# Making the folded key weights in both row halves on TensorE, with smaller weight loads and a new order

## Chip, cores, metric

The kernel runs on one core of a Trainium2 chip. The metric is device time in microseconds of one launch; a number of runs is given by its median, lowest and highest. Lower is better. Line numbers (L390) are those of the kernel before.

## What is computed

The input x has S = 2048 rows of D = 576. There are 32 heads of 18 columns. Cut to what matters:

```python
def _A_ref(x, wqkv, w_phi, wo):          # token mixer
    q, k, v = split_heads(x @ wqkv)
    pq = einsum("bhsd,hdf->bhsf", q, w_phi)
    pk = einsum("bhsd,hdf->bhsf", k, w_phi)
    phi_q = concat([softmax(pq), softmax(-pq)], -1)
    phi_k = concat([softmax(pk), softmax(-pk)], -1)
    kv = einsum("bhsf,bhsd->bhfd", phi_k, v)
    z  = einsum("bhsf->bhf", phi_k)
    o = (phi_q @ kv) / (phi_q @ z + 1e-6)
    return merge_heads(o) @ wo

def _B_ref(x, w1, b1, w2, b2):           # MLP, 576 -> 4608 -> 576
    return gelu(layernorm(x) @ w1 + b1) @ w2 + b2

h  = x + _A_ref(layernorm(x), ...)
h2 = h + _B_ref(layernorm(h), ...)
```

## The kernel before, in words

The 2048 rows are 16 tiles of 128 rows; two tiles make a pair p (0 to 7), the unit of the first part. The contraction of 576 is cut into KC = 9 chunks of 64. In `lnb` the chunks of a pair's two tiles stand beside each other, so that one 128x128 transpose brings chunk c of tile 0 to partitions 0 to 63 and of tile 1 to partitions 64 to 127 (`lnT`). Every projection (`project`, L390) then runs two rows of 64 partitions at once, one tile in each, 18 matmuls with 288 columns; its weights are needed in both halves of the partitions.

The feature weights are folded: wk times the block-diagonal w_phi (`bd`, made by `spread`, L198, on GpSimd from w_phi and a mask). For that wk is transposed on TensorE in five column groups (`flip_mm` L334, evicted by `flip_ev` L340 into `wT`), and `fold_mm` (L350) multiplies in 128-row chunks, six matmuls each, evicted by `fold_ev` (L361) into `wkp` for keys and `wqp` for queries. A 128-row chunk holds two 64-row chunks, each in one half; so the other halves are filled by copies (`swap` L368, `swap_last` L371, on GpSimd, VectorE and ScalarE for keys; `swap_q` by DMA for queries), and key and query projections pick their chunks in the order CROSSED. The value weights `wv` are loaded into the lower half and copied to the upper half on GpSimd (`copy_values`, L158).

Order of the first part, per pair and half i of the columns:
- `stats` (L271 to L274, VectorE), `power` (L279, GpSimd), `centre` (L245, GpSimd) and `scale` (L291 on VectorE or L251 on ScalarE) normalise the rows; the turn to `lnT` is done by TensorE for pairs 0 and 1 (`turn_x_mm`, L308, evicted at L315 and L317) and by a transposing DMA for the rest (`turn_dma`, L298).
- `key_mm` and `value_mm` (L390), `key_exp` (two exponentials, L412, ScalarE), `value_ev` (L400), `key_sum` (reduce and reciprocal, L441 and L443, VectorE), `key_weigh` (two multiplies of a tile, L447, GpSimd), and `sums` (L482, TensorE), which adds the pair to `acc_kv`, a PSUM tile that lives through the whole first part.
- After the last `sums`, `table` (L495, L499) makes the masked matrix `kvm` with `window_masks` (L217, L221); queries run through the same steps (`query_*`), are turned by DMA (`turn_q`), and `combine_mm` (L565), `divide` (L575, L578), the turn of o, `residual_mm` (L612), `residual_add` (L625, L626), `second` (L631, L233, L235) and `rescale` (L239) lead to the MLP's input `ln2T`.

PSUM in the first part: the pool `two` has three buffers of two banks, taken in turn by every product and transpose; `pn` has one.

Then come eight MLP blocks of 256 rows (`mlp`): `up` makes 18 pairs of hidden chunks (`pair`, L1027; gelu on ScalarE, L1051) and `down` multiplies back (L1072; last add L1076). Between them stand the next rows' combines and residuals, at places given by `rises` and `falls` (index of the pair, or of the matmul). In the first block `up` begins with the first of the two row tiles alone for `first` = 3 pairs, before the second tile's turn has arrived.

The order on each engine is written out by hand: the list of calls L682 to L1008 is the program order, and every engine runs its own instructions in that order and waits at each for what it reads. Loads are issued by SP (`load_*`), apart from x tiles 0 and 1 and w_phi, which ScalarE issues first of all (L162 to L170). SP's queue also holds the transposing DMAs. Eight completion semaphores serve the DMAs of SP and ScalarE in turn, so each DMA waits for the one eight places ahead of it.

## Time and profile before

| what | value |
|---|---|
| three runs: median (lowest to highest) | 402.1 us (401.37 to 405.12) |
| the profiled execution: time, span | 403.26 us, 401.5 us |
| mean granted clock of TensorE in it | 0.991 |
| first matmul starts | 1.42 us |
| first key projection starts | 19.04 us |
| last sums end | 72.6 us |
| first whole pair of the MLP starts | 95.93 us |
| last matmul ends | 398.1 us |

The profile gives for each engine the time in which it is busy: PE is TensorE's matmuls, PEld its weight loads, DVE VectorE, ACT ScalarE, POOL GpSimd, SP SyncE; a "q" behind a name is the queue that issues. A line of the timeline has start, duration, engine, line, operation, output and inputs, count, and in brackets the idle time before it with what ended it; instructions of one kind that follow each other are merged, and the shape shown is that of the first. The granted clock is the share of TensorE's clock that was let through.

### The profile page before, as it was taken

The page shows a single profiled execution, that of the slowest core. Times are in us where ns is not written, and L with a number is a line of the kernel's source. Part 1 is how long each engine was busy: PE and PEld are TensorE (multiplying, and loading weights), DVE is VectorE, ACT ScalarE, POOL GpSimd, SP SyncE. Part 2 cuts the span into 40 slices and gives each one's busy share as a digit, 9 for nine tenths or more (in the row PEclk, how much of TensorE's full clock was granted, in tenths as well). Part 3 has the DMA queues.
Part 4 walks back from the last instruction along what each step waited for, and adds up shares of the span by engine and source line. Part 5 has one row for each costly group of instructions (what it writes and reads, how often), then busy time and mean ns, then how long its engine had stood idle before and what let it go on. Part 6 is the DMA issues. An engine that isn't in the chain of part 4 may idle for free.

```text
span 401.5 us, 12158 instructions
## 1 busy us (share of the span) xinstructions
PE 387.7 (97%) x5435; PEld 322.4 (80%) x5435; DVE 166.7 (42%) x353; ACT 186.4 (46%) x399; POOL 124.1 (31%) x139
## 2 busy tenths in 40 slices
PE   7699999988999999999999999999999999999996
PEld 6577777768877898888778888888888888778875
DVE  4898996467118307500750264036205300600000
ACT  2888887765800680077008601840383048106800
POOL 4999899117303302500250034003401100211010
PEclk9899999999999999999999999999999999999999
DMA  8998759999963602350332034004400500120000
GB/s 204 183 172 177 128 108 191 220 202 230 304 82 75 105 4 38 66 77 2 60 65 56 2 75 85 23 3 84 94 3 2 104 16 2 21 56 16 2 16 16
DMA packets 72462, 33.84 MB, mean 84 GB/s; under 512 B 58842, under 2 KB 69338, under 8 KB 72410
## 3 DMA queue, kind: packets, MB, share of 16 engines
q1 hardware_dynamic: 71520, 32.75, 41.6%
q8 instruction: 42, 0.69, 0.7%
q10 hardware_dynamic: 890, 0.32, 0.4%
q14 instruction: 10, 0.08, 0.1%
HBM read 16.53 MB, written 2.36 MB: 47 GB/s over the span
## 4 chain that ended last, share of the span: by engine, by line
PE 86%; DVE 5%; DMA 4%; POOL 1%; ACT 1%; issue 1%; ACTq 0%; SPq 0%; DVEq 0%; POOLq 0%
PE ph L1027 35%; PE po L1072 33%; PE pk L390 7%; PE pa L612 4%; PE pv L390 4%; DMA w<-in_A_w_phi_dram 2%; PE acc_kv L482 1%; PE pn L565 1%; DMA lnT<-shared 1%; DVE st L626 1%; DVE xh L625 1%; DVE shared L239 1%; DVE st L271 1%; PE pT L308 1%; POOL wv L158 1%
## 5 line engine op out<-in xcount | busy, mean ns | idle before, releaser
L1051 ACT ACTIVATE h<-ph,b1col 128x256 bf16<-128x256 f32 x288 | 120.7, 471 | 170.6 <-PE ph L1027 153.7
L1027 PE MATMUL ph<-shared,w 64*128 64x256 bf16 (+1 forms) x2646 | 145.1, 268 | 2.9 <-DVE shared L315 1.1
L1072 PE MATMUL po<-w,h 128*128 128x288 bf16 x1152 | 144.7, 286 | 0.0
L1027 PEld LDWEIGHTS <-w 64*128 64x128 bf16 x2646 | 128.6, 95 | 18.6 <-issue 5.5
L1072 PEld LDWEIGHTS <-h 128*128 128x128 bf16 x1152 | 111.2, 98 | 29.3 <-issue 1.9
L235 POOL TENSOR_TENSOR rs<-va,mhalf 128x1 f32<-128x1 f32 x16 | 8.8, 551 | 173.2 <-DVE va L233 173.2
L625 DVE TENSOR_TENSOR xh<-pa,xh 128x288 bf16<-128x288 f32 x32 | 14.3, 446 | 114.7 <-PE pa L612 114.7
L390 PEld LDWEIGHTS <-lnT 64*128 64x128 bf16 x864 | 42.3, 95 | 12.9 <-issue 1.4
L1076 DVE TENSOR_TENSOR ot<-po,hb 128x288 bf16<-128x288 f32 x32 | 14.5, 454 | 80.6 <-PE po L1072 79.8
L447 POOL TENSOR_TENSOR phiq<-phiq,rk 128x576 bf16<-128x576 bf16 x32 | 36.4, 1164 | 22.2 <-DVE rk L443 22.2
L1062 POOL TENSOR_TENSOR hb<-xh,b2bc 128x576 f32<-128x576 bf16 x16 | 20.4, 1275 | 62.9 <-DVE ot L1076 61.2
L447 POOL TENSOR_TENSOR phik<-phik,rk 128x576 bf16<-128x576 bf16 x32 | 36.3, 1164 | 1.5 <-DVE rk L443 1.3
L441 DVE TENSOR_REDUCE sk<-phik 128x64 f32<-128x1152 bf16 x16 | 21.3, 1332 | 1.9 <-ACT phik L412 1.8
L412 ACT ACTIVATE phiq<-pk 128x576 bf16<-128x576 f32 x32 | 18.6, 651 | 7.5 <-PE pk L390 7.5
L441 DVE TENSOR_REDUCE sk<-phiq 128x64 f32<-128x1152 bf16 x16 | 21.3, 1330 | 0.0
L390 PE MATMUL pv<-wv,lnT 64*128 64x288 bf16 x288 | 20.5, 289 | 0.7 <-POOL wv L158 0.5
L390 PE MATMUL pk<-shared,lnT 64*128 64x288 bf16 x288 | 19.8, 283 | 0.6 <-DMA lnT<-shared 0.4
L412 ACT ACTIVATE phik<-pk 128x576 bf16<-128x576 f32 x32 | 18.8, 664 | 3.3 <-PE pk L390 3.3
L390 PE MATMUL pk<-wqp,lnT 64*128 64x288 bf16 x288 | 19.4, 283 | 0.2 <-DVE xh L625 0.2
L612 PE MATMUL pa<-wo,shared 64*128 64x288 bf16 x288 | 19.0, 283 | 0.0
L443 DVE RECIPROCAL rk<-sk 128x64 f32<-128x64 f32 x32 | 17.7, 553 | 2.2
L612 PEld LDWEIGHTS <-shared 64*128 64x128 bf16 x288 | 14.5, 94 | 3.2 <-issue 0.2
(71 smaller groups left out, 199.5 us busy)
## 6 DMA issues: line engine op xcount, KB each, us to landing
w<-in_B_w_dram SPq DMA_DIRECT2D x24, 432.0 KB, 7.9
...
```

Source lines behind the costliest of these rows:

```text
L390: nc.tensor.matmul(dst[:, a, 0:HALF], lhs[rows, c, :], w[rows, slot, i * HALF : (i + 1) * HALF], start=(n == 0), stop=(n == KC - 1),)
L412: nc.scalar.activation(rows[:, :, i * HH : (i + 1) * HH, s, :], flight[key, p, i][:, :, 0:HALF].rearrange("p a (h f) -> p a h f", f=DH), A ...
L441: nc.vector.tensor_reduce(sk[:, :, :], part_of(dst, i), AX.X, ALU.add)
L443: nc.vector.reciprocal(rk[:, :, :], sk[:, :, :])
L447: eng.tensor_tensor(part, part, flight["r" + key, p, i][:, a, :].rearrange("p (h o) -> p h o", o=1).to_broadcast([P, NH, DH]), ALU.mult,)
L612: nc.tensor.matmul(pa[a], oT[p % 2][rows, c, :], wo[rows, c, cs], start=(c == 0), stop=(c == KC - 1),)
L625: nc.vector.tensor_tensor(xh[:, t, cs], flight["a", p, i][a], xh[:, t, cs], ALU.add)
L1027: nc.tensor.matmul(ph[half][:, cols], w1[p_ // 9][rows, c, p_ % 9 * P : (p_ % 9 + 1) * P], x[rows, c, cols], start=(c == 0), stop=(c == KC ...
L1051: nc.scalar.activation(h1[m // 9][:, m % 9, :], ph[half][:, :], AF.Gelu_apprx_tanh, bias=b1col[:, m : m + 1], scale=1.0,)
L1062: nc.gpsimd.tensor_tensor(hb[:, :], xh[:, t, :], b2bc[:, :], ALU.add)
L1072: nc.tensor.matmul(po[:, :], h1[m // 9][:, m % 9, i_ * P : (i_ + 1) * P], w2[m // 18][:, m % 18, cs], start=(n == 0), stop=(n == NM - 1),)
L1076: nc.vector.tensor_tensor(ot[:, cs], po[:, :], hb[:, cs], ALU.add)
```

## The change

- `load_wk` loads wk's columns in two pieces (254 and 322) and its last 64 rows apart; `load_rows` goes. All are issued by SP, ahead of the x tiles from 2 on.
- w_phi's two DMAs are issued by GpSimd, behind the identity matrix.
- `fold_k_mm` folds keys in nine chunks of 64 rows, each twice with the same operands, once into output partitions 0 to 63 and once into 64 to 127; `fold_k_ev` evicts both at once. The key swaps go, and keys use the plain order of chunks.
- `stats` takes one tile at a time, and the variance plus epsilon is made on GpSimd. `copy_values` copies five or four chunks at a time. `sums` takes one tile at a time. `sk` and `rk` have six buffers instead of three.
- Transposes into the pool `two` take two buffers, one for each part.
- In the first MLP block only one pair begins with the first row tile alone, behind the second tile's turn on TensorE; `enter` of the next rows comes at 60 instead of 64; the second weighing of query pair 3 and its turn move from the end of block 0 into block 1.
- The order of the first part is new throughout. Of it the diff below shows the start, up to the load of the last x tiles, and the end, from the last `sums` on; in the part left out the same steps stand in another order. On SP the order of loads is then: wk pieces, x 2 to 3, x 4 to 7, values 0, x 8 to 11, values 1, wq, the turn of pair 2, five turns of wq, the turn of pair 3, x 12 to 15, and so on.

```diff
@@ -138,11 +138,14 @@
-    def load_rows(dst, src):
-        n = src.shape[1]
-        nc.sync.dma_start(dst[0:64, 4, 0:n], src[512:576, :])
+    def load_wk(part):
+        if part == 0:
+            nc.sync.dma_start(wk[0:KH, 4, :], A_wqkv[512:D, D : 2 * D])
+            return
+        f0, f1 = ((0, 254), (254, D))[part - 1]
         nc.sync.dma_start(
-            dst[:, 0:4, 0:n], src[0:512, :].rearrange("(c p) f -> p c f", p=P)
+            wk[:, 0:4, f0:f1],
+            A_wqkv[0:512, D + f0 : D + f1].rearrange("(c p) f -> p c f", p=P),
         )
...
@@ -153,24 +156,24 @@
             ),
         )
 
-    def copy_values(i, copy):
+    def copy_values(i, part, copy):
         cs = slice(i * HALF, (i + 1) * HALF)
-        copy(wv[KH:P, :, cs], wv[0:KH, :, cs])
+        ks = slice(part * 5, 5 + part * 4)
+        copy(wv[KH:P, ks, cs], wv[0:KH, ks, cs])
 
     wphi_rows = A_w_phi.rearrange("h d f -> (h d) f")
+
+    def load_x(t0, t1):
+        nc.sync.dma_start(xh[:, t0:t1, :], x_v[:, t0:t1, :])
+
     for t in range(2):
         nc.scalar.dma_start(xh[:, t, :], x_v[:, t, :])
 
-    def load_x(t0, t1):
-        nc.sync.dma_start(xh[:, t0:t1, :], x_v[:, t0:t1, :])
-
-    nc.scalar.dma_start(
+    make_identity(nc, ident)
+    nc.gpsimd.dma_start(
         wph[0:126, 0:4, :], wphi_rows[0:504, :].rearrange("(g p) f -> p g f", p=126)
     )
-    nc.scalar.dma_start(wph[0:72, 4, :], wphi_rows[504:576, :])
-    load_rows(wk, A_wqkv[:, D : 2 * D])
-
-    make_identity(nc, ident)
+    nc.gpsimd.dma_start(wph[0:72, 4, :], wphi_rows[504:576, :])
     ones7 = small.tile([P, 7], FP32, name="ones7", tag="ones7")
     nc.gpsimd.memset(ones7[:, :], 1.0)
     nc.gpsimd.memset(mhalf[:, :], -0.5)
...
@@ -263,15 +266,18 @@
     def turned(p):
         return lnT[p // 2][:, p % 2, :, :]
 
-    def stats(p):
-        mv = small.tile([P, 2, 2], FP32, name="mv", tag="mv")
-        for i in range(2):
-            st = small.tile([P, 2, nc.vector.BN_STATS_DIM], FP32, name="st", tag="st")
-            for h in range(2):
-                nc.vector.bn_stats(st[:, h, :], xh[:, 2 * p + i, h * HALF : (h + 1) * HALF])
-            nc.vector.bn_aggr(mv[:, i, :], st[:, :, :])
+    def stats(p, i):
+        if i == 0:
+            moments[p] = [small.tile([P, 2, 2], FP32, name="mv", tag="mv")]
+        mv = moments[p][0]
+        st = small.tile([P, 2, nc.vector.BN_STATS_DIM], FP32, name="st", tag="st")
+        for h in range(2):
+            nc.vector.bn_stats(st[:, h, :], xh[:, 2 * p + i, h * HALF : (h + 1) * HALF])
+        nc.vector.bn_aggr(mv[:, i, :], st[:, :, :])
+        if i == 0:
+            return
         va = small.tile([P, 2], FP32, name="va", tag="va")
-        nc.vector.tensor_scalar(va[:, :], mv[:, :, 1], 1.0, EPS, ALU.mult, ALU.add)
+        nc.gpsimd.tensor_scalar(va[:, :], mv[:, :, 1], 1.0, EPS, ALU.mult, ALU.add)
         moments[p] = [mv, va, None, None]
 
     def power(p):
...
     flight = {}
 
-    def transposes(key, src, home=two, tag="two"):
-        pT = flight[key] = home.tile([P, 16, P], BF16, name="pT", tag=tag)
+    def transposes(key, src, home=None):
+        if home:
+            pT = home.tile([P, 16, P], BF16, name="pT", tag="pn")
+            parts = [pT[:, 0:5, :], pT[:, 8:12, :]]
+        else:
+            parts = [
+                two.tile([P, 5 - e, P], BF16, name="pT", tag="two")[:, :, :] for e in range(2)
+            ]
+        flight[key] = parts
         for c in range(KC):
             nc.tensor.transpose(
-                pT[:, c + c // 5 * 3, :], src[:, c * P : (c + 1) * P], ident[:, :]
+                parts[c // 5][:, c % 5, :], src[:, c * P : (c + 1) * P], ident[:, :]
             )
 
     def turned_back(key, dst, part, copy):
-        pT = flight[key]
-        if part == 0:
-            copy(dst[:, 0:5, :], pT[:, 0:5, :])
-        else:
-            copy(dst[:, 5:KC, :], pT[:, 8:12, :])
+        copy(dst[:, 5 * part : 5 + 4 * part, :], flight[key][part])
 
     def turn_x_mm(p):
         transposes(("x", p), lnb[p % 3][:, :, :, :].rearrange("p c a k -> p (c a k)"))
...
         nc.sync.dma_start_transpose(wT[:, :, c * P : (c + 1) * P], wq[:, c, :])
+
+    def fold_k_mm(c):
+        pW = flight["k", c] = two.tile([P, 2, 512], FP32, name="pW", tag="two")
+        for i, off, g, lo, hi in BITS:
+            k = P if g < NG - 1 else 72
+            for a in range(2):
+                nc.tensor.matmul(
+                    pW[a * KH : (a + 1) * KH, i, off : off + hi - lo],
+                    wT[:k, g, c * KH : (c + 1) * KH],
+                    bd[:k, g, :, :].rearrange("p h f -> p (h f)")[:, lo:hi],
+                    start=True, stop=True,
+                )
+
+    def fold_k_ev(c, copy):
+        copy(
+            wkp[:, c, :].rearrange("p (i f) -> p i f", i=2), flight["k", c][:, :, 0:HALF]
+        )
 
     def fold_mm(name, c):
         m = P if c < NC - 1 else 64
...
-    folded = {"k": wkp, "q": wqp}
+    folded = {"q": wqp}
...
-    def swap(c0, c1, up, copy):
...
-    def swap_last(copy):
...
     def key_mm(p, i):
-        features("k", wkp, p, i)
+        features("k", wkp, p, i, PLAIN)
...
     def query_mm(p, i):
-        features("q", wqp, p, i)
+        features("q", wqp, p, i, CROSSED)
...
-        sk = small.tile([P, 2, NH], FP32, name="sk", tag="sk")
+        sk = small.tile([P, 2, NH], FP32, name="sk", tag="sk", bufs=6)
...
-    def sums(p):
-        for a in range(2):
...
+    def sums(p, a):
+        t = 2 * p + a
+        left.remove(t)
...
+    load_wk(1)
+    load_wk(0)
+    warm(50)
+    flip_mm(0)
+    load_wk(2)
+    load_x(2, 4)
+    load_x(4, 8)
+    window_masks()
+    flip_ev(0, act)
+    load_values(0)
+    load_x(8, 12)
+    load_values(1)
+    load_wq()
+    stats(0, 0)
+    flip_mm(1)
+    stats(0, 1)
+    power(0)
+    flip_mm(4)
+    flip_ev(1, dve)
+    centre(0, 0)
+    scale(0, 1, vec)
+    scale(0, 0, act)
+    spread(2)
+    flip_mm(3)
+    flip_ev(3, act)
+    spread(4)
+    spread(0)
+    flip_ev(4, dve)
+    flip_mm(2)
+    stats(1, 0)
+    flip_ev(2, act)
+    turn_x_mm(0)
+    turn_x_ev(0, 0, dve)
+    turn_x_ev(0, 1, act)
+    spread(3)
+    spread(1)
+    fold_k_mm(3)
+    ones()
+    fold_k_ev(3, act)
+    fold_k_mm(5)
+    fold_k_ev(5, act)
+    stats(1, 1)
+    power(1)
+    fold_k_mm(6)
+    fold_k_ev(6, dve)
+    copy_values(0, 0, gps)
+    stats(2, 0)
+    scale(1, 1, vec)
+    stats(2, 1)
+    power(2)
+    fold_k_mm(0)
+    fold_k_ev(0, act)
+    scale(1, 0, vec)
+    fold_k_mm(8)
+    fold_k_ev(8, act)
+    stats(3, 0)
+    fold_k_mm(7)
+    fold_k_ev(7, act)
+    fold_k_mm(4)
+    scale(2, 0, vec)
+    fold_k_ev(4, act)
+    stats(3, 1)
+    scale(2, 1, vec)
+    copy_values(0, 1, gps)
+    fold_k_mm(2)
+    fold_k_ev(2, act)
+    fold_k_mm(1)
+    turn_x_mm(1)
+    fold_k_ev(1, act)
+    turn_x_ev(1, 0, act)
+    copy_values(1, 1, gps)
+    power(3)
+    turn_dma(2)
+    turn_x_ev(1, 1, act)
+    stats(4, 0)
+    copy_values(1, 0, gps)
+    key_mm(0, 0)
+    turn_wq(2)
+    centre(3, 0)
+    key_exp(0, 0)
+    key_sum(0, 0)
+    key_weigh(0, 0, 1, pool)
+    key_mm(0, 1)
+    key_exp(0, 1)
+    turn_wq(1)
+    value_mm(0, 0)
+    value_ev(0, 0, act)
+    key_mm(1, 0)
+    key_exp(1, 0)
+    turn_wq(3)
+    key_weigh(0, 0, 0, pool)
+    centre(3, 1)
+    stats(4, 1)
+    value_mm(1, 0)
+    power(4)
+    centre(4, 1)
+    key_sum(1, 0)
+    value_mm(1, 1)
+    key_weigh(1, 0, 0, pool)
+    value_mm(0, 1)
+    key_weigh(1, 0, 1, pool)
+    turn_wq(4)
+    value_ev(1, 0, act)
+    scale(3, 0, act)
+    value_mm(2, 1)
+    value_ev(1, 1, act)
+    stats(5, 0)
+    scale(3, 1, act)
+    turn_wq(0)
+    value_ev(0, 1, act)
+    turn_dma(3)
+    load_x(12, 16)
...
+    sums(6, 1)
+    query_mm(1, 0)
+    key_weigh(7, 0, 1, pool)
+    value_ev(7, 0, dve)
+    key_weigh(7, 1, 0, pool)
+    load_w1(0, 3)
+    key_weigh(6, 1, 0, pool)
+    sums(6, 0)
+    sums(7, 0)
+    key_weigh(7, 1, 1, pool)
+    sums(7, 1)
+    table()
+    close_keys()
+    query_exp(5, 1)
+    query_exp(1, 0)
+    query_mm(1, 1)
+    query_mm(6, 0)
+    query_exp(1, 1)
+    turn_q(0)
+    combine_mm(1, two)
+    combine_mm(0)
+    query_mm(6, 1)
+    query_exp(6, 0)
+    divide(1)
+    query_exp(6, 1)
+    divide(0)
+    turn_o_mm()
+    query_mm(3, 1)
+    turn_o_ev(1, dve)
+    turn_o_ev(0, act)
+    load_wo(2)
+    load_w1(0, 2)
+    residual_mm(0, 0, double_bank())
+    residual_add(0, 0, 1)
+    residual_add(0, 0, 0)
+    query_exp(3, 1)
+    query_mm(4, 1)
+    residual_mm(0, 1, double_bank())
+    residual_add(0, 1, 0)
+    query_exp(4, 1)
+    second(0)
+    query_mm(2, 1)
+    query_exp(2, 1)
+    query_mm(7, 0)
+    residual_add(0, 1, 1)
+    second(1)
+    query_mm(7, 1)
+    load_w1(1, 0)
+    load_w2(0, 5)
+    rescale(0, 1)
+    rescale(0, 0)
+    query_exp(7, 0)
+    rescale(1, 0)
+    rescale(1, 1)
+    turn2_mm(0)
+    turn2_ev(0, 1, dve)
+    turn2_ev(0, 0, dve)
+    load_w2(0, 0)
+    load_w1(1, 1)
+    query_exp(7, 1)
+    load_w1(1, 3)
+    load_w2(0, 4)
+    load_w1(1, 4)
+    gelu_table()
+    load_w1(1, 5)
+    load_w1(1, 2)
+    load_w2(0, 3)
+    load_w2(0, 2)
+    load_w2(0, 1)
+    close_weights()
+    turn_b1_mm()
+    turn_b1_ev(act)
...
@@ -1034,9 +1076,6 @@
             return [acc.tile([P, TB], FP32, name="ph", tag="acc") for _ in range(2)]
 
         begun = [banks_of() for _ in range(first)]
-        if first == 3:
-            a, b, c = begun
-            begun = [[a[0], c[0]], [a[1], c[1]], b]
         for p_ in range(first):
             pair(begun[p_], p_, slice(0, P))
             if p_ == 0:
@@ -1096,10 +1135,12 @@
                 15: lambda: combine(2 * a),
                 17: lambda: turn_q(b),
             }
-        rise = up(s_, rises, 3 if s_ == 0 else 0)
+        if s_ == 1:
+            rises[3] = lambda: (norm_q(b, 1), turn_q(b))
+        rise = up(s_, rises, 1 if s_ == 0 else 0)
         if s_ == 0:
+            turn2_mm(1, pn_pool)
             next(rise)
-            turn2_mm(1, pn_pool, "pn")
             for part in range(2):
                 turn2_ev(1, part, dve)
             for q in (a, b):
@@ -1110,9 +1151,8 @@
         h1 = next(rise)
         if s_ == 0:
             falls = {
-                0: lambda: leave(a), 64: lambda: enter(a), 84: lambda: combine(2 * b),
+                0: lambda: leave(a), 60: lambda: enter(a), 84: lambda: combine(2 * b),
                 96: lambda: norm_q(c, 0), 118: lambda: leave(b),
-                126: lambda: (norm_q(c, 1), turn_q(c)),
             }
         else:
             if a < NS:
```

390 lines of the change are left out of this document (138 added, 252 removed).

## The prediction

> **What bounds the kernel now.** I read the page first (busy shares and slices), then the windows of ten and of one microsecond, then the timelines of the stretches where TensorE stops.
>
> ```profile
> span 401.5 us, 12158 instructions
> ...
> PE 387.7 (97%) x5435; PEld 322.4 (80%) x5435; DVE 166.7 (42%) x353; ACT 186.4 (46%) x399; POOL 124.1 (31%) x139
> ```
>
> TensorE is the bound: 13.8 us of 401.5 are idle. 1.4 lie before its first instruction and 3.4 behind its last, so 9.0 us lie inside. The windows say where.
>
> ```profile
> 10.00:20.00 10.00, 6.90 (x86) 5.38 (x85) 8.90 (x29) 8.22 (x14) 9.40 (x13) 0.83 1.03 184
> 20.00:30.00 10.00, 9.17 (x146) 7.55 (x145) 9.28 (x16) 8.21 (x16) 9.76 (x10) 1.00 0.99 172
> ...
> 80.00:90.00 10.00, 8.15 (x126) 6.24 (x123) 6.51 (x18) 6.66 (x11) 1.12 (x2) 0.94 1.07 209
> 90.00:100.00 10.00, 8.94 (x186) 7.99 (x186) 7.93 (x10) 5.62 (x14) 6.75 (x7) 0.89 1.05 225
> 100.00:110.00 10.00, 10.00 (x188) 8.72 (x184) 1.18 (x3) 7.99 (x21) 3.49 (x4) 1.00 1.07 307
> ```
>
> The columns are length, busy time of PE, PEld, DVE, ACT and POOL, granted clock, DMA share, GB/s. Idle are 5.5 us before 30, and 2.9 from 80 to 100; from 100 on only 0.4 (at 134). The clock is low in the same places.
>
> ```profile
> 14.00:15.00 1.00, 1.00 (x13) 0.85 (x11) 0.90 (x4) 1.00 (x3) 0.92 (x2) 0.50 1.23 168
> ...
> 90.00:91.00 1.00, 1.00 (x18) 0.81 (x18) 0.56 (x2) 0.00 (x0) 0.00 (x0) 0.50 1.02 151
> ```
>
> The granted clock is 0.50 from 13.9 to 17.1 and from 88.9 to 92.2, each time after some 3.4 us in which TensorE was busy about half. "Busy" there hides lost time.
>
> ```profile
> 8.28 1.01 PE L334 MATMUL pX<-ident,w 128*128 128x128 bf16 x15 [1.35 <-DMA w<-in_A_wqkv_dram]
> ...
> 9.49 1.53 POOL L198 TENSOR_TENSOR w<-w,mask 126x126 bf16<-126x126 bf16 x4 [4.74 <-DMA w<-in_A_w_phi_dram]
> ...
> 12.47 0.87 PE L350 MATMUL pW<-w 128*128 128x36 bf16 x16 [1.18 <-POOL w L198]
> ...
> 19.04 3.50 PE L390 MATMUL pk<-shared,lnT 64*128 64x288 bf16 x54
> ...
> 26.95 2.38 PE L390 MATMUL pk<-shared,lnT 64*128 64x288 bf16 x36 [0.36 <-DMA lnT<-shared]
> ```
>
> This is the front: the turns of wk wait for its load until 8.28, the folds wait for w_phi (9.49) and the last spread (12.42), the first key projection starts at 19.04. At 26.95 seven projections are done and the eighth starts. From there to the last sums (end 72.6) TensorE pauses for 0.24 us only.
>
> **The change, part by part.** I call a projection 18 matmuls of line 390; one takes 1.10 us from start to start.
>
> *Flips.* SP now issues wk in three pieces ahead of everything, w_phi leaves ScalarE's queue. x tiles 0 and 1 and wk's first piece with its last rows are 0.63 MB; at the 255 GB/s of 2 to 10 us (2.04 MB in 8) they land by 5, the second piece by 6.5. The 50 warm-up transposes end at 6.9, so the wait of 1.35 us goes. Flips are then paced by evictions: ACT copies groups 0, 3, 2 (0.64 each) around one scale (0.87), DVE groups 1 and 4 (0.45 to 0.64). wT is whole at 10.1.
>
> *w_phi.* No row shows a DMA issued from GpSimd. Bounds: 2.6 us from issue to landing (x on ScalarE's queue) and, above, the 7.8 us that w_phi took (1.68 to 9.49). Its 576 rows of 36 bytes shared the DMA engines with wk and landed 1.2 us behind it; wk is now earlier by about 1.8, so 9.5 - 1.8 = 7.7, and 0.2 for an issue that comes later: I take 7.9, near the upper end. Spreads, 5 x 0.4 behind it, end at 9.9. First fold: 10.1 (10.1 to 11.5).
>
> *Folds.* 30 wide matmuls for the key weights become 108 narrow ones (64 columns out). Six narrow and six wide ran from 35.87 to 36.56; six wide alone take 0.37 (40.36 to 40.73); so six narrow take 0.32, a fold of twelve 0.63, nine folds 5.7, against 1.9 before.
>
> ```profile
> 35.87 0.84 PE L350 MATMUL pW<-w 128*64 128x126 bf16 x12
> 36.56 0.86 PE L482 MATMUL acc_kv<-vals,phik 128*128 128x76 bf16 x18
> ...
> 40.36 0.44 PE L350 MATMUL pW<-w 128*128 128x126 bf16 x6
> 40.73 1.28 PE L390 MATMUL pk<-shared,lnT 64*128 64x288 bf16 x18
> ```
>
> Eight evictions on ACT (0.64) and one on DVE keep that pace. The last fold ends at 15.8; the turn of x pair 1 (0.68) covers its eviction. First key projection 16.6, against 19.04. Bounds: 0.37 a fold (halves wholly side by side) would be paced by ACT at 5.1 us and save 0.6; 95 ns a matmul (the weight-load row, nothing hidden) gives 10.3 us.
>
> The swaps go: POOL 3 x 1.14, DVE 0.45, ACT 0.67; all stood before or beside the first keys.
>
> *Up to the eighth projection.* Seven at 1.10 end at 24.3, against 26.95. What can be late: POOL copies the values halves (2 x 2.35 in four pieces); the copies wait for the second load, landing by 17 at 200 GB/s, and end at 20.1; the projection that needs the last piece starts at 21. The transposing DMA of pair 2 waits for DVE's scale at 18.7 and took 3.7 (median) to 5.05: 22.4 to 23.8, in time. That of pair 3 now stands behind five turns of wq on SP's queue (1.31 each): issued 26.7, landed 30.4, needed at 29.8. Gain 2.65 - 0.6, plus the 0.24 at 44.9: 2.2, keeping 0 to 3.
>
> *Variances* on POOL: 8 x 0.27, DVE gives up 8 x 0.37. POOL matters: it weighs from 24.8 to 70.9, 86 to 100% busy in each ten. In the new order the weighing starts at 21.6 (after the first key sum), and 36 weighs at 1.164 with four rounds of variance and power (0.97) and six shifts (0.27) behind it make 47.4: 69.0. TensorE needs the last at 70. The window masks (1.1) move to POOL's idle start, from behind the last weigh, where they cost nothing. Nothing for both.
>
> *Middle.* From the last sums (72.60) to the fourth pair of the first MLP block (95.93) are 23.3 us: eight query projections, two combines, turns, two residual halves and three pairs.
>
> ```profile
> 87.93 0.21 PE L1027 MATMUL ph<-shared,w 64*128 64x128 bf16 x1 [1.08 <-DVE shared L315]
> 88.50 0.82 PE L1027 MATMUL ph<-shared,w 64*128 64x128 bf16 x17 [0.36 <-ACT phiq L412]
> ...
> 95.93 4.32 PE L1027 MATMUL ph<-shared,w 64*128 64x256 bf16 x76 [1.06 <-issue]
> ```
>
> Counted anew from the last sums (0): two queries to 2.2; table on DVE to 1.5; combines to 3.05; one query to 4.15, where before there were two, so TensorE waits for the divides until 5.15 (new idle: 1.0); turn, query, residual, query, residual to 10.3; three queries to 13.6. Meanwhile adds, statistics (3.7 with the second's aggregate now ahead) and rescales (1.04) on DVE end at 14.1, so the turn starts at 14.15 (idle 0.55) and ends at 14.85. DVE rescales the second tile before it evicts the first (15.15, then 0.42 + 0.49): the first pair starts at 16.05, its second half at 17.0. Only this pair is now cut into halves (each half 0.85 against 0.5 for half a whole pair), instead of three. Fourth pair: 19.9. The 1.06 "issue" gap has no releaser; half of it is kept: 20.4. Gain 23.3 - 20.4 = 2.9. It includes 1.6 for the half clock, which I expect to be gone: in the last 3.4 us before the first pair TensorE is busy 70%, against 45%. Bounds: 1.3 if the half clock stays, 3.5 without the gap.
>
> *Later.* The weighing of query pair 3 leaves the end of the first block, where DVE's sum (1.27 + 0.55) held the last output add and TensorE 0.37 us: gain 0.4. In block 1 it is needed some 20 us after its new place. SP's loads of the last weights start as much earlier as TensorE.
>
> *Sum.* 2.2 + 2.9 + 0.4 = 5.5. The profiled execution took 403.26 us (span 401.5 and 1.8 around it), 1.2 above the median of the runs, 402.1. So 397.8 from the one, 396.6 from the other; I say 397.
>
> A rule of the Trainium skill against this change: "DMA: Bandwidth & Descriptors", Specifications, puts line rate at 512 bytes and more, and the first piece of wk has rows of 508. Our row is milder: wq's 252-byte rows moved in a window of 184 GB/s, large rows at 307; for 0.26 MB that is 0.6 us, mostly under the warm-up transposes.
>
> **Rivals.**
>
> *Narrow folds cost a whole weight load each.* At 95 ns instead of 52 nine folds take 10.3 us, the first key comes at 21.2, 2.2 later than now: front -2.2 instead of +2.2, and 5.5 - 4.4 leaves 401. For it: PEld's row (95 ns). Against it: the six narrow ones from 35.87 ran at 52. The Trainium skill, "TensorEngine Tiling (Array Packing)", Restrictions, says that column tiling switches the fast weight load off, which would speak for this rival. Chance 0.08.
>
> *Front gain lost:* w_phi lands as late as before or up to 2 us later (9.5 to 11.5). The folds start at 11.5 to 13.5, TensorE idles long enough for the half clock: front +0.8 to -1.5, total 398.5 to 401. The same size comes if the reordered middle part (25 to 70) has an eviction that holds a bank. Chance 0.22.
>
> *Middle gain lost:* half clock and gap both remain: 5.5 - 2.1 gives 399. For it: two new idle stretches (1.0, 0.55). Chance 0.18.
>
> *Slower: POOL's queue.* Its copy of the second values half waits for a load that is now behind 3.1 MB; behind that copy stand a power, a copy, a shift and all 36 weighs, 3.3 us before the first weigh. Landing by 18 costs nothing; each further us moves the table by one once 1 us of slack is used. From 24.5 on it eats the whole 5.5, which needs 130 GB/s (3.1 MB by then) where the first slices show 172 to 204; landing at 28.5 gives 406.5. DMAs that GpSimd issues ahead of all this, if they hold its queue, work the same way. Chance 0.10, taken whole as slower by over 1%.
>
> **Numbers.** Forecast 0.42: 397, its own range 395.5 to 398. Within 1% of 402.1 (398.1 to 406.1; about what a measurement of this kernel can tell from no change) lie most of the front and middle rivals and the fold rival. Faster by over 1%: 0.48 (the forecast, and 0.06 of the middle rival where only one of its two parts comes); same 0.42 (0.22 + 0.08 + 0.12); slower 0.10. Range 394.5 to 402.5: below lies the front at its bound of 3, the gap gone and the folds at theirs; above, the slower rival and the worst of the front one.
>
> **What would show it.** First line-343 transpose at 6.9; spreads from 8; first key projection near 16.6; eighth at 24.3; POOL's last key weigh by 70; last sums end near 70.4; no 0.50 clock at the first pairs; fourth pair about 20.4 later; no idle at the end of block 0. Wrong if the first spread is past 9.5, if a fold takes over 0.8, or if weighs start after 22.5.

## The result, and the profile after

The changed kernel takes 400.04 us (median of 13 runs, 399.53 to 402.53), the kernel before 402.60 us beside it (13 runs, 400.35 to 405.12): ratio 0.9941, 95% interval 0.9918 to 0.9964. It is faster by about 2.4 us, not by the 5.5 forecast. The profiled executions took 403.26 us (before) and 400.94 us (after, span 399.2); each is 0.7 to 0.9 above its median. The ratios, here and in the table below, are taken over fast runs alone (two far slower ones, of 506 and 809 us, are left out) and are not the quotient of the medians. Line numbers are from here on those of the changed kernel (projections L409, sums L503, weighs L466).

The page of the changed kernel, its span and its busy times:

```profile
span 399.2 us, 12230 instructions
...
PE 385.8 (97%) x5477; PEld 320.9 (80%) x5477; DVE 165.6 (41%) x347; ACT 186.3 (47%) x399; POOL 123.4 (31%) x147
```

TensorE still bounds the kernel. Its busy time is 1.9 us shorter, though it has 42 matmuls more: 78 more narrow folds (108 for 30), 36 fewer in the split pairs. The windows of ten microseconds (columns as before):

```profile
10.00:20.00 10.00, 7.42 (x164) 5.95 (x165) 8.70 (x25) 7.80 (x14) 6.04 (x9) 1.00 0.88 163
20.00:30.00 10.00, 9.57 (x156) 8.62 (x154) 8.76 (x16) 8.42 (x15) 9.48 (x14) 1.00 0.98 122
...
80.00:90.00 10.00, 8.91 (x145) 7.83 (x143) 6.91 (x18) 7.08 (x12) 1.10 (x2) 1.00 1.07 220
90.00:100.00 10.00, 9.96 (x195) 9.58 (x197) 7.93 (x10) 7.58 (x20) 7.16 (x7) 1.00 1.05 223
```

The granted clock is 1.00 where it was 0.83 and 0.89: both stretches of half clock are gone, so TensorE does more in less busy time. The idle time from 10 to 20 is 2.6 us and from 80 to 90 still 1.1; from 90 to 100 it fell from 1.1 to 0.04.

The timeline of TensorE in the front (start, duration, then what ran, with the idle time before it in brackets):

```profile
5.61 0.72 PE L343 MATMUL pX<-ident,w 128*128 128x128 bf16 x10
7.95 1.03 PE L343 MATMUL pX<-ident,w 128*72 128x128 bf16 x15 [1.61 <-DMA w<-in_A_wqkv_dram]
...
9.97 3.95 PE L359 MATMUL pW<-w 128*64 128x126 bf16 x108 [0.16 <-ACT w L349]
15.22 0.68 PE L321 MATMUL pT<-ident,shared 128*128 128x128 bf16 x9 [1.30 <-DVE shared L297]
15.83 1.52 PE L409 MATMUL pk<-shared,lnT 64*128 64x288 bf16 x21
18.37 1.14 PE L409 MATMUL pk<-shared,lnT 64*128 64x288 bf16 x15 [1.01 <-issue]
...
23.37 3.46 PE L409 MATMUL pv<-wv,lnT 64*128 64x288 bf16 x53 [0.43 <-POOL wv L162]
...
31.75 1.28 PE L409 MATMUL pv<-wv,lnT 64*128 64x288 bf16 x18 [0.51 <-DMA lnT<-shared]
```

The 108 narrow folds take 3.95 us, and the first key projection starts at 15.83 (19.04 before, 16.6 forecast). Then come four waits: 1.01 named "issue" (its releaser is not in the profile), 0.43 for GpSimd's copy of value weights, 0.51 for pair 3's landing, and 0.78 for pair 6's at 53.9. The wait for the copy is not new; the kernel before has it too:

```profile
23.12 1.26 PE L390 MATMUL pv<-wv,lnT 64*128 64x288 bf16 x17 [0.47 <-POOL wv L158]
```

From the first key to the last sums TensorE is idle for 2.74 us, against 1.08 before (0.47 for that copy, 0.36 for a landing, 0.24 for ScalarE).

GpSimd in the same stretch:

```profile
7.55 1.73 POOL L201 TENSOR_TENSOR w<-w,mask 126x126 bf16<-126x126 bf16 x5
...
14.52 1.38 POOL L162 COPY wv<-wv 64x1440 bf16<-64x1440 bf16 x1 [1.88 <-DMA wv<-in_A_wqkv_dram]
...
18.62 0.19 POOL L280 TENSOR_SCALAR va<-mv 128x2 f32<-128x2 f32 x1 [1.67 <-DVE mv L276]
18.88 2.23 POOL L162 COPY wv<-wv 64x1152 bf16<-64x1152 bf16 x2
...
21.94 1.38 POOL L162 COPY wv<-wv 64x1440 bf16<-64x1440 bf16 x1
...
23.64 2.28 POOL L466 TENSOR_TENSOR phik<-phik,rk 128x576 bf16<-128x576 bf16 x2
```

GpSimd stands idle twice, 3.55 us together, first for the values load and then for VectorE's aggregate. The last copy of value weights ends at 23.3 (20.1 forecast), and the first weigh starts at 23.64 (21.6 forecast).

The middle, from the turn of o to the first pair of the MLP:

```profile
78.36 0.68 PE L321 MATMUL pT<-ident,ob 128*128 128x128 bf16 x9 [0.85 <-DVE ob L599]
79.55 1.28 PE L409 MATMUL pk<-wqp,lnT 64*128 64x288 bf16 x18 [0.52 <-DVE shared L326]
...
87.92 0.68 PE L321 MATMUL pT<-ident,shared 128*128 128x128 bf16 x9 [0.47 <-DVE shared L242]
89.21 0.17 PE L685 MATMUL pb<-ident,b1nat 36*128 36x36 bf16 x1 [0.61 <-DVE shared L326]
...
89.92 10.31 PE L1069 MATMUL ph<-shared,w 64*128 64x128 bf16 x195
```

Four waits, 2.45 us. No gap follows in the pairs up to 100; before, 1.06 us named "issue" lay in the fourth pair.

### The profile page after: what moved, and what is told of

It is laid out like the page before. It is cut to its first block, busy times and chain, and to the rows that moved or that the text cites. A ratio compares the mean times of both kernels' runs of the same rounds, so it can differ in the third digit from the quotient of the medians.

```text
span 399.2 us, 12230 instructions
## 1 busy us (share of the span) xinstructions
PE 385.8 (97%) x5477; PEld 320.9 (80%) x5477; DVE 165.6 (41%) x347; ACT 186.3 (47%) x399; POOL 123.4 (31%) x147
## 4 chain that ended last, share of the span: by engine, by line
PE 83%; POOL 6%; DMA 4%; DVE 2%; issue 1%; ACT 1%; SPq 1%; POOLq 0%
PE ph L1069 36%; PE po L1111 36%; PE pa L633 4%; PE pk L409 4%; POOL phik L466 3%; DMA wv<-in_A_wqkv_dram 3%; PE pn L586 1%; DMA lnT<-shared 1%; POOL wv L162 1%; PE pv L409 1%; POOL rs L285 1%; PE acc_kv L503 1%; ACT phik L431 1%; DVE shared L242 0%; ACT shared L254 0%
## 5 line engine op out<-in xcount | busy, mean ns | idle before, releaser
L1069 PE MATMUL ph<-shared,w 64*128 64x256 bf16 (+1 forms) x2610 | 143.5, 268 | 0.0
L1069 PEld LDWEIGHTS <-w 64*128 64x128 bf16 x2610 | 127.1, 94 | 15.8 <-issue 2.0
L409 PEld LDWEIGHTS <-lnT 64*128 64x128 bf16 x864 | 43.0, 94 | 13.4 <-issue 2.5
L466 POOL TENSOR_TENSOR phiq<-phiq,rk 128x576 bf16<-128x576 bf16 x32 | 36.4, 1163 | 21.9 <-DVE rk L462 16.6
L466 POOL TENSOR_TENSOR phik<-phik,rk 128x576 bf16<-128x576 bf16 x32 | 36.2, 1162 | 0.9 <-ACT vals L419 0.9
L409 PE MATMUL pk<-shared,lnT 64*128 64x288 bf16 x288 | 20.1, 283 | 1.8 <-issue 1.0
L409 PE MATMUL pv<-wv,lnT 64*128 64x288 bf16 x288 | 20.4, 283 | 0.9 <-DMA lnT<-shared 0.5
L409 PE MATMUL pk<-wqp,lnT 64*128 64x288 bf16 x288 | 19.5, 283 | 0.5 <-DVE shared L326 0.5
```

The lines of the kernel that those rows point to most:

```text
L409: nc.tensor.matmul(dst[:, a, 0:HALF], lhs[rows, c, :], w[rows, slot, i * HALF : (i + 1) * HALF], start=(n == 0), stop=(n == KC - 1),)
L466: eng.tensor_tensor(part, part, flight["r" + key, p, i][:, a, :].rearrange("p (h o) -> p h o", o=1).to_broadcast([P, NH, DH]), ALU.mult,)
L1069: nc.tensor.matmul(ph[half][:, cols], w1[p_ // 9][rows, c, p_ % 9 * P : (p_ % 9 + 1) * P], x[rows, c, cols], start=(c == 0), stop=(c == KC ...
```

## The experiments

The table has the profiled execution of each kernel: start of the first key projection, start of the first weigh, end of the last key weigh, end of the last sums, and the time from there to the start of the fourth pair. Then the median of the runs and the ratio to the kernel before on the same chip, with its interval. Ratios of different groups were taken on different chips, so intervals that overlap rank nothing. The first five columns are of one execution each, and they scatter: changed, e2_first, e7_warm, e11_wphi, e16_shift and e17_onetile have the same order up to the last sums, and their last sums end anywhere from 71.14 to 73.27 and their first weighs start from 22.05 to 23.64. A shift of less than that shows nothing.

| kernel | first key | first weigh | last weigh ends | last sums end | to 4th pair | median us | ratio |
|---|---|---|---|---|---|---|---|
| before | 19.04 | 24.82 | 70.93 | 72.67 | 21.09 | 402.60 | |
| changed | 15.83 | 23.64 | 70.58 | 73.14 | 19.95 | 400.04 | 0.9941 (0.9918 to 0.9964) |
| e1_mid | 19.99 | 25.77 | 71.98 | 74.26 | 19.19 | 401.48 | 0.996 (0.994 to 0.998) |
| e2_first | 15.55 | 22.38 | 69.94 | 72.49 | 21.67 | 402.50 | 0.9988 (0.997 to 1.0006) |
| e3_sums | 15.15 | 22.28 | 69.12 | 72.16 | 19.94 | 400.11 | 0.9917 (0.9889 to 0.9946) |
| e4_values | 15.18 | 22.00 | 69.50 | 72.05 | 19.94 | 399.81 | 0.9932 (0.991 to 0.9955) |
| e5_turns | 15.70 | 23.16 | 69.28 | 71.83 | 19.92 | 399.58 | 0.991 (0.9884 to 0.9936) |
| e6_var | 16.15 | 21.82 | 69.33 | 71.88 | 19.95 | 400.48 | 0.9941 (0.9916 to 0.9966) |
| e7_warm | 16.78 | 23.61 | 70.71 | 73.27 | 19.95 | 400.78 (1 run) | |
| e8_all | 15.30 | 22.36 | 68.45 | 71.48 | 19.92 | 399.26 | 0.9914 (0.9884 to 0.9944) |
| e9_best | 18.66 | 25.72 | 74.60 | 75.19 | 21.63 | 402.83 | 0.9977 (0.9955 to 0.9999) |
| e10_bestvar | 18.26 | 23.96 | 73.65 | 74.07 | 20.59 | 402.00 | 0.9973 (0.9943 to 1.0004) |
| e11_wphi | 15.56 | 22.39 | 69.96 | 72.52 | 19.95 | 399.92 | 0.9897 (0.9868 to 0.9926) |
| e12_fill | 16.59 | 23.42 | 70.92 | 71.34 | 20.59 | 398.68 | 0.988 (0.9851 to 0.9908) |
| e13_turnfill | 15.45 | 22.51 | 69.53 | 69.95 | 20.59 | 398.37 | 0.9887 (0.9868 to 0.9906) |
| e14_best | 15.67 | 22.73 | 68.49 | 69.78 | 20.62 | 399.29 | 0.9918 (0.9889 to 0.9947) |
| e15_dve | 18.89 | 25.48 | 70.12 | 72.00 | 20.59 | 400.65 | 0.9945 (0.9923 to 0.9966) |
| e16_shift | 16.04 | 22.86 | 69.85 | 72.41 | 20.15 | 400.12 (1 run) | |
| e17_onetile | 15.22 | 22.05 | 68.59 | 71.14 | 19.82 | 399.71 | 0.9929 (0.9904 to 0.9954) |
| e18_best | 15.40 | 22.96 | 68.81 | 69.23 | 21.11 | 398.68 | 0.9906 (0.9872 to 0.9939) |

### The two halves of the change: e1_mid and e2_first

e1_mid is the kernel before with the changed kernel's order behind the last sums (its query numbers fitted to what is left there) and its new MLP begin; e2_first is the changed kernel with the old one:

```diff
e1_mid, on the kernel before:
-        rise = up(s_, rises, 3 if s_ == 0 else 0)
+        rise = up(s_, rises, 1 if s_ == 0 else 0)
-        0: lambda: leave(a), 64: lambda: enter(a), ...
+        0: lambda: leave(a), 60: lambda: enter(a), ...
```

> The kernel before, with only the middle of the change (the order behind the last sums, one begun pair instead of three, the weighing of query pair 3 moved into block 1). Theory A: all of the gain is made there, the first part only breaks even (its last sums end at 73.1 against 72.6). Then this kernel gains as much as the whole change or a little more, 2.5 to 3 us, ratio 0.993 to 0.994, and the fourth pair starts about 20.4 us behind the last sums. Theory B: half the gain comes from the first part, and the middle is worth 1 to 1.5 us: ratio 0.997.

> The changed kernel with the middle of before (three begun pairs, both queries between combine and turn of o, the weighing back in block 0). Theory A: time of the kernel before within 0.5 us, ratio 0.999 to 1.002. Theory B: 1 to 1.5 us faster than before, ratio 0.997. If the half clock is what made the middle dear, it shows again at the first pairs.

e1_mid gives 0.996 (1.6 us), e2_first 0.9988 (0.5 us, an interval that holds no change). Together they give 0.9948, close to the whole change's 0.9941. So by these ratios the middle, with the new begin of the MLP, brought two thirds of what came, and the front, whose first key is 3.2 us earlier, brought nothing that can be told from no change. The intervals are too wide to decide between the theories A and B.

With the old middle the half clock is back in the profiled execution of e2_first, from 89.2 to 92.6; with the new one, in e1_mid, these microseconds have 1.00. The window of e2_first (columns as before):

```profile
90.00:91.00 1.00, 1.00 (x15) 0.80 (x14) 0.11 (x1) 0.36 (x2) 0.00 (x0) 0.50 1.05 196
```

From the last sums to the fourth pair the new middle takes 1.9 us less in e1_mid than in the kernel before, and 1.7 less in the changed kernel than in e2_first. But the half clock is not what makes the old middle slow in the end: ten of e2_first's twelve runs have a mean granted clock of 1.000, and their median is 402.5 us as well.

### Where the front's gain goes: e3_sums, e4_values, e5_turns

e3_sums puts the two tiles' sums of a pair side by side, e4_values asks for the values loads two places earlier, e5_turns asks for two transposing DMAs earlier:

```diff
e3_sums, for every pair:
-    sums(0, 0)
     key_mm(3, 0)
     ...
+    sums(0, 0)
     sums(0, 1)
e4_values:
-    load_x(4, 8)
+    load_values(0)
...
-    load_values(0)
+    load_x(4, 8)
+    load_values(1)
     load_x(8, 12)
-    load_values(1)
e5_turns:
+    centre(3, 1)          # ahead of the first weighs
...
+    scale(3, 1, act)
+    turn_dma(3)           # ahead of the last two turn_wq
...
+    scale(6, 1, act)
+    turn_dma(6)           # ahead of load_w1(0, 4)
...                        # each of these goes from its old place further down
```

> The changed kernel with both tiles' sums of a pair side by side again (the first of the two moved to the second). Theory M: each switch between the 64-row tiling of the projections and the full array costs TensorE about 0.1 us (a projection ahead of sums takes 1.20 instead of 1.10, nine sums alone 0.45 instead of 0.40), so five groups fewer give 0.6 to 1.0 us by the last sums and in the total: ratio to before 0.992. Rival: TensorE waits for GpSimd's weighs in any case; then the switches are hidden, the last sums end at 73 and the ratio stays at 0.994.

> The changed kernel with the two value-weight loads issued two places earlier, each ahead of a load of x tiles. Theory P: GpSimd's queue is what the first part waits for: its copy of the values stood until 14.5 for a load and everything behind it, so that the first weigh came at 23.6 instead of 21.6. Then the copies end 1.5 to 2 us earlier, the first weigh starts by 22, and 1 us or more is left at the last sums: ratio to before 0.991. Rival: TensorE's own stops (an instruction gap, the turns of pairs 3 and 6, the switches) set the pace, the first weigh comes earlier and the last sums do not: 0.994.

> The changed kernel with two transposing DMAs asked for earlier: that of x pair 3 ahead of the last two turns of wq (its two scales and shifts move up with it), and that of pair 6 ahead of the first MLP weight's load, with its second scale. Theory A (the front's gain is lost in waits for these two landings, 0.51 and 0.78 us in the changed kernel's trace): both waits go, the last sums end 1.3 us earlier, near 71.8, and the time falls by about 1.3 us, to a ratio of 0.991 to the kernel before. Theory B (the landings are only the last of several late things; GpSimd's weighing holds the last sums): the waits go, but the last sums end within 0.5 us of 73.1 and the time stays.

A projection followed by a projection takes 1.10 us from start to start, one followed by sums or a fold 1.20 to 1.21; the changed kernel has 12 of these from its eighth projection to the last sums, the kernel before 9, e3_sums 8. In that stretch, without the idle times, the changed kernel takes 46.38 us and e3_sums 45.77: the split of the sums costs 0.6 us. The Trainium skill, "TensorEngine Tiling (Array Packing)", Key Properties, says that a change of tiling mode drains TensorE. The trace agrees: projections run in two row tiles, sums and query folds on the full array, and each step from the former to the latter costs 0.1 us.

In e5_turns both waits for landings are gone, and the next one is there:

```profile
57.68 0.52 PE L503 MATMUL acc_kv<-vals,phik 128*128 128x76 bf16 x9
58.91 1.28 PE L409 MATMUL pk<-shared,lnT 64*128 64x288 bf16 x18 [0.70 <-DMA lnT<-shared]
```

The key projection of pair 7 now waits 0.70 us for its landing: its scales stand behind three sums on VectorE, the DMA is issued at 52.13, and it lands 6.8 us later. The last sums end at 71.83, as theory A had it, and in e4_values the first weigh starts at 22.00, as theory P had it; both lie about where kernels without these edits have them too (71.14 and 22.05 in e17_onetile). The intervals of all three overlap with the changed kernel's, so none of the edits is told from it by its time.

### Variances, warm-up, queue of w_phi, and all at once: e6_var, e7_warm, e11_wphi, e8_all

```diff
e6_var:
-        nc.gpsimd.tensor_scalar(va[:, :], mv[:, :, 1], 1.0, EPS, ...)
+        nc.vector.tensor_scalar(va[:, :], mv[:, :, 1], 1.0, EPS, ...)
e7_warm:
-    warm(50)
+    warm(42)
e11_wphi, both loads:
-    nc.gpsimd.dma_start(wph...
+    nc.scalar.dma_start(wph...
```

e8_all is e3_sums, e4_values and e5_turns in one.

> The changed kernel with the variance's one operation per pair back on VectorE. Theory A (GpSimd and VectorE wait on each other in the front: 1.67 us of idle GpSimd for the variance's input behind the copies of the values weights): first weigh earlier by 0.5 us or more, last key weigh earlier by 8 x 0.27 = 2.2 us at most, last sums 0.5 to 1 us earlier. Theory B (as predicted, variances cost nothing in either place): last sums within 0.4 us of 73.1, the time within 0.5 us of the changed kernel's.

> The changed kernel with 42 warming transposes in place of 50, so that 16 fewer TensorE instructions (a weight load and a matmul each) stand ahead of everything. Theory A (the gap of 1.01 us named issue, inside a key projection at 17.4, is a fetch of instructions, and lies at a fixed count of TensorE's instructions, the 449th): the gap moves 8 matmuls further on in the program, or goes where its packet is in time. Theory B (it belongs to that place in the program: an eviction, a bank or a landing): it stays at the same matmul. The time itself is not expected to change by more than 0.5 us.

> The changed kernel with the feature weights' two loads (w_phi) back on ScalarE's queue, behind x tiles 0 and 1. Theory A (they landed late because wk's large load was ahead of them, and GpSimd's queue only keeps ScalarE free): they land within 0.7 us of the changed kernel's 7.5, and the time stays within 0.5 us. Theory B (the queue is what brought them in early): they land 1.5 us or more later, as in the kernel before (9.4), the first fold comes 1 us or more behind the end of the flips, and the time rises by 0.5 to 1.5 us.

> The changed kernel with three edits at once: both tiles' sums of a pair side by side, the values loads two places earlier, and the two transposing DMAs asked for earlier. If the three costs are separate (switches between row tiles and the full array about 0.5, values 0.4, landings 1.3), the last sums end near 71.0 and the time is near 398, a ratio of 0.988. If one limit is behind all three (GpSimd's weighing, which ends at 69 to 70.6 in all of them), the last sums stay near 72 and the time near 399.5.

e6_var starts weighing at 21.82 instead of 23.64, as its theory A said (but 22.05 came without this edit, too), and the ratio is the same, 0.9941: in either place the variances cost nothing that shows. In e11_wphi the spreads start at 7.80 instead of 7.55 and the time does not rise: w_phi is early because wk is early, not because of GpSimd's queue. In e8_all the last sums end 1.7 us earlier than in the changed kernel, though the wait for pair 7's landing grew to 1.64 us; its time overlaps with e3_sums and e5_turns. In e7_warm the gap of 1.01 us did not occur; e16_shift, below, decides that.

### TensorE or GpSimd: e12_fill, e9_best, e10_bestvar

e12_fill moves two query projections of the changed kernel behind the last sums, where TensorE waits for VectorE anyway. e9_best is e8_all with that and with pair 7's landing asked for earlier; e10_bestvar adds e6_var.

```diff
e12_fill (in e9_best too):
-    query_mm(5, 1)
-    query_mm(1, 0)
...
     table()
     close_keys()
+    query_mm(5, 1)
+    query_mm(1, 0)
...
     combine_mm(1, two)
     combine_mm(0)
+    query_mm(1, 1)
...
+    query_mm(6, 0)
...
     turn_o_mm()
...
e9_best:
     power(7)
...
+    scale(7, 1, vec)
+    scale(7, 0, vec)
+    turn_dma(7)
     key_sum(5, 0)
```

> The changed kernel with two query projections (tile pair 5's second half and pair 1's first) taken from ahead of the last sums and put behind them, one more between the combines and the turn of o, one more ahead of the first pair. Theory A (GpSimd's last key weigh, at 70.6, is not what TensorE waits for; TensorE's own work and the middle's chain of VectorE steps are): the last sums end near 71.1 instead of 73.1, the middle's idle time falls from 2.45 to about 0.5 us, and the time falls by 1.5 to 2 us. Theory B (the weighing is the limit): TensorE waits for the last weighs, the last sums end near 73 or the wait equals what was moved, and the time falls by less than 0.5 us.

> The changed kernel with all the edits together: sums of a pair side by side, values loads two places earlier, the transposing DMAs of pairs 3, 6 and now also 7 asked for earlier (with their scales), and two query projections moved behind the last sums. From the kernel with the first three (span 397.2): its wait of 1.64 us for pair 7's landing goes, and the middle's idle of 2.4 us falls to about 0.5; if GpSimd is no limit the span is 393.7 and the time near 396 (ratio 0.984). If GpSimd's weighing holds the last sums (its weighs end at 68.5 there), TensorE waits some 1.5 us for it at the last sums and the time is near 397.5.

> The same as the kernel with all edits, and the variances back on VectorE. If GpSimd's weighing is the limit by now, its end comes up to 2.2 us earlier (8 x 0.27) and the time falls by up to 1 us against the one with all edits; if TensorE alone is, the time is the same within 0.5 us.

e12_fill is the one edit that stands clear of the changed kernel: 0.988, interval 0.9851 to 0.9908. Its TensorE timeline at the last sums and behind:

```profile
69.49 1.85 PE L503 MATMUL acc_kv<-vals,phik 128*128 128x76 bf16 x36
71.28 2.38 PE L409 MATMUL pk<-wqp,lnT 64*128 64x288 bf16 x36
...
76.74 0.68 PE L321 MATMUL pT<-ident,ob 128*128 128x128 bf16 x9
77.93 1.28 PE L409 MATMUL pk<-wqp,lnT 64*128 64x288 bf16 x18 [0.52 <-DVE shared L326]
```

The wait of 0.85 before the turn of o is gone, the middle's idle time falls from 2.45 to 1.03, and the last sums end at 71.34, right behind the last weigh (70.92) and without a wait over 0.3 us. So two limits lie close together here: TensorE's work with its waits (73.14 in the changed kernel) and GpSimd's weighing (70.58, plus 0.45 for the last sums).

e9_best shows what happens when the second is passed. TensorE, then GpSimd, then VectorE of that kernel:

```profile
73.54 1.65 PE L503 MATMUL acc_kv<-vals,phik 128*128 128x76 bf16 x23 [3.57 <-POOL phik L466]
```

```profile
50.58 0.70 POOL L285 TENSOR_TENSOR rs<-va,mhalf 128x2 f32<-128x2 f32 x1
54.39 6.77 POOL L466 TENSOR_TENSOR phik<-phik,rk 128x576 bf16<-128x576 bf16 x6 [3.10 <-PE pk L409]
```

```profile
51.32 1.05 DVE L297 TENSOR_SCALAR shared<-xh,mv,rs 128x576 bf16<-128x576 bf16 x2 [4.54 <-DMA wqp<-wqp]
52.29 1.34 DVE L460 TENSOR_REDUCE sk<-phik 128x64 f32<-128x1152 bf16 x1
```

The scale of pair 7 stands ahead of a key sum on VectorE and waits for the power that GpSimd makes only at 50.58, behind its weighs. (The brackets name other releasers; by the times, the scale starts where the power ends, and the weigh where the key sum behind it and its reciprocal do.) Meanwhile no key sum is made, so GpSimd has nothing to weigh for 3.10 us. TensorE's wait of 3.57 us at the last sums holds this, but not this alone: in this execution the first weigh also started late, at 25.72. e10_bestvar has the same order of the scale, the same 3.10 us on GpSimd and a time that cannot be told from e9_best's; there the waits at the last sums are 0.80 and 0.25, and 1.63 us were lost before, on pair 4's landing.

### Mended, and GpSimd relieved: e13_turnfill, e14_best, e15_dve

```diff
e13_turnfill and e14_best, on e9_best:
-    scale(7, 1, vec)      # ahead of key_sum(5, 0)
-    scale(7, 0, vec)
-    turn_dma(7)
     key_sum(5, 0)
...
     key_sum(3, 1)
+    scale(7, 1, vec)
+    scale(7, 0, vec)
+    turn_dma(7)
     key_sum(5, 1)
e15_dve, on e14_best:
-    key_weigh(7, 1, 0, pool)
+    key_weigh(7, 1, 0, vec)
```

e13_turnfill has the changed kernel's order of sums and loads, e14_best that of e3_sums and e4_values.

> The changed kernel with the transposing DMAs of pairs 3, 6 and 7 asked for earlier (pair 7's scales now between two key sums, behind the power that they need) and the two query projections behind the last sums. Theory A (the landings' waits and the middle's idle are separate losses of TensorE): 0.991 from the landings and 0.988 from the queries add up, 0.985 or about 397 us. Theory B (GpSimd takes over: first weigh at 23, 46 us of weighing, its end at 69.3): TensorE waits 1 to 2 us for the last weighs, and the time is that with the queries alone, 0.988.

> As the one before, with sums side by side and the values loads two places earlier too: the first kernel with all edits (whose GpSimd stood idle for 3.1 us, since VectorE waited for a power with two key sums behind it) with that wait mended. Theory A (that idle stretch was the cause of the 3.57 us wait at the last sums): the wait falls to 1.5 us or less, the time to 397.5 or less. Theory B (the earlier loads or the grouping of the sums are the cause): the wait stays above 2.5 us and the time near 402.

> As the mended kernel with all edits, with one of the last key weighs (pair 7, second half, tile 0) on VectorE in place of GpSimd. If GpSimd's weighing is the limit of the last sums, they end up to 1.16 us earlier and the time falls by 0.5 to 1.1 us against the one before; if TensorE is, nothing moves.

With the scales two sums later the wait for GpSimd is gone in both, and e14_best's ratio is 0.9918 where e9_best's is 0.9977: theory A of e14_best, though its 399.29 us miss the 397.5 expected. e13_turnfill's ratio is 0.9887, e12_fill's 0.988: the earlier landings add nothing that can be told on top of the queries. They could not: in e13_turnfill pair 4's landing is late now (1.13 us), in e14_best too (1.58). e15_dve missed: no gain, and a front that began 3 us late in the profiled execution, with VectorE waiting 1.52 us for the load of x tiles where e14_best, with the same code up to there, waited 0.38. How late these loads land differs between executions, and what sets it was not found. One thing stands out: the three late fronts (first key at 18.26 to 18.89 in e9_best, e10_bestvar and e15_dve) are all among the six kernels that ask for the value weights two places earlier, while none of the twelve with the changed kernel's order of loads is past 16.78. The other three of the six have their first key at 15.18 to 15.67, so this is a suspicion and not shown.

### The gap without a releaser: e16_shift

```diff
     flip_mm(0)
+    warm(20)
     load_wk(2)
```

> The changed kernel with 20 more warming transposes behind the first flip, where TensorE waits anyway: 40 more TensorE instructions ahead of everything else. Theory A (gaps named issue lie at fixed counts of TensorE's instructions, 193 behind a multiple of 256): a gap, where one shows, is at the 449th or a later such count, now 20 matmuls earlier in the program; none at the place of the changed kernel's. Theory B (that place in the program): a gap at the same matmul, the 12th of the second key projection, now the 489th instruction.

```profile
16.04 0.29 PE L409 MATMUL pk<-shared,lnT 64*128 64x288 bf16 x1
17.91 2.36 PE L409 MATMUL pk<-shared,lnT 64*128 64x288 bf16 x35 [1.58 <-issue]
```

In the changed kernel the gap came behind 21 matmuls of the first keys, here behind one: 20 transposes more ahead, 20 matmuls earlier in the program. Counted in the trace, 449 TensorE instructions precede it both times. That is 193 more than a multiple of 256. (The matmul behind the gap of the changed kernel is the 4th of the second key projection, not the 12th as the expectation has it.) The other gaps named "issue" stand behind 1987 (e10_bestvar, e14_best, e15_dve), 2754 (before, e1_mid), 3009 (e3_sums, e10_bestvar, e14_best) and 3011 (e12_fill), 193 to 195 more than a multiple. So it belongs to a count, not to a place: theory A.

### The turn's tiles, and the best kernel again: e17_onetile, e18_best

```diff
-            parts = [
-                two.tile([P, 5 - e, P], BF16, name="pT", tag="two")[:, :, :] for e in range(2)
-            ]
+        pT = (home or two).tile([P, 16, P], BF16, name="pT", tag="pn" if home else "two")
+        parts = [pT[:, 0:5, :], pT[:, 8:12, :]]
```

> The changed kernel with a turn's nine transposes in one tile of the pool two again, as in the kernel before, in place of one tile for each part. Theory A (the split takes two of the pool's three tiles, so that the projection behind the turn of o and the small transpose behind the second turn wait for VectorE's eviction, 0.52 and 0.61 us in the changed kernel's trace, while the kernel before's middle with the new order showed none and 0.16): both waits go, from the last sums to the fourth pair 19.95 becomes 19.0 to 19.3, and the time falls by 0.7 to 1 us, to a ratio of 0.992. Theory B (the middle is a chain of VectorE's steps and the waits only move): the same stretch stays within 0.3 us of 19.95, with the waits at the second turn instead.

> The kernel with the early landings and the two queries behind the last sums, and the turns in one tile again. Its two waits in the middle (0.51 behind the turn of o, 0.52 at the small transpose) go if the split made them: 1 us off, to 397.4 or a ratio of 0.986. If VectorE's chain is the limit, the second turn starts no earlier and the ratio stays at 0.9887.

Theory A's waits go, and another takes their place. TensorE of e17_onetile:

```profile
86.19 0.19 PE L680 MATMUL pb<-ident,b1nat 36*128 36x36 bf16 x1
...
87.99 4.24 PE L1064 MATMUL ph<-shared,w 64*128 64x128 bf16 x92 [0.77 <-ACT b1col L683]
```

The split made the two waits of 0.52 and 0.61, but behind them stands ScalarE: five exponentials, the table load for gelu (1.28 us) and the eviction of b1 must end before the first pair. The stretch is 19.82 instead of 19.95. In e18_best that wait is 1.54 and the ratio, 0.9906, no better than e13_turnfill's. The length is that of theory B, but the chain that sets it is ScalarE's and not VectorE's.

## Why the prediction was wrong

The forecast was 2.2 (front) + 2.9 (middle) + 0.4 (later) = 5.5 us; about 2.4 came. Between the two profiled executions the front, up to the last sums, brought -0.5, the middle 1.1, and what lies behind the start of the fourth pair 1.6, of which 1.06 are the gap named "issue" that the changed kernel did not have there.

- **Flips, w_phi, folds: right or better.** Flips started at 5.6 (6.9), the spreads at 7.55 (8), the first fold at 9.97 (10.1). Only the wait for wk did not go: its second piece was there at 7.95 (6.5 forecast), 1.61 us late, covered by the earlier end of the warm-up. A fold took 0.44 us instead of 0.63: it is near the lower bound of 0.37 given there, the halves run side by side. The first key came at 15.83 (16.6), although TensorE then waited 1.30 us for VectorE's scale.
- **The step that failed: the front's gain is carried on unchanged.** From the first key to the last sums I let TensorE pause for 0.6 us and take 53.8 us (16.6 to 70.4); it took 57.3. Of the 3.5 us, 2.1 are waits (2.74 instead of 0.6), and 0.5 the further switches between row tiles and the full array, which I did not cost at all. The other 0.9 belong to the waits, too: from one projection's start to the next it takes longer than 1.10 us where a wait lies between, even when the idle time in the brackets is taken off. With the two waits among the first seven it is 1.28 us each, and 1.21 for the projection behind the gap (together 0.5 more); with the landings of pairs 3 and 6 it is 1.37 and 1.27 (0.4 more). "In time" for the landing of pair 2 was right; pair 6's, which the prediction never looked at, was 0.78 late. That the step failed does not hang on this one execution: the other kernels with the changed front and all their queries ahead of the last sums take 55.7 to 57.0 us for the stretch. e5_turns, e8_all, e13_turnfill and e14_best show the next landing late when one was moved.
- **GpSimd's queue.** Its length was right (46.9 us from first to last weigh; 47.4 forecast), its start was not: 23.64 instead of 21.6, as the four copies wait for their load (1.88 us) and share the queue with powers and variances that wait for VectorE (1.67). So the prediction's own sign "weighs start after 22.5" came. With the last weigh at 70.58 the last sums could not have ended before 71.0, whatever TensorE did. "Nothing" for the variances themselves stands (e6_var).
- **Middle: the new length was right, the old one misread.** I measured the old kernel to 95.93, the restart behind the gap in the fourth pair; that pair began at 93.76, so 2.2 us of the 23.3 did not belong to the stretch. The new middle was put at 19.9 without a gap and took 19.95. From the last sums to its start the gain is 21.09 - 19.95 = 1.1 us, and the gap of 1.06 is met or missed by chance. The half clock went, as said, but its price of 1.6 us is not borne out: e2_first, with the old middle, is no faster in the ten runs without it. Of the new idle time I had 1.55 us; it is 2.45, since I did not see that two tiles for a turn hold two of the pool's three buffers (0.52 and 0.61).
- **Later: right.** The idle 0.37 us at the end of the first block is gone.

Of the rivals the front one came nearest: 398.5 to 401, "front gain lost", though by the gap, landings, a copy and switches and not by a late w_phi or an eviction. The middle rival's 399 is near as well, but neither of its conditions came: half clock and gap were both gone. The fold rival fell with its rule. The Trainium skill, "TensorEngine Tiling (Array Packing)", Restrictions, says that column tiling switches the fast weight load off; here 108 narrow matmuls took 36.6 ns each, less than the 94 ns of a weight load's row, so no such cost is seen.

What stays open: the first key's start varies from 15.2 to 18.9 us between kernels with nearly the same code ahead of it (15.67 and 18.89 in e14_best and e15_dve, where it is the same), with the landings of wk and x. And the landings' waits were never removed all together, so their worth in the time is not measured.
